# Splitting all seven output products of five head groups on two levels, with five running sums that share two places and wait in DRAM

## The chip, the cores and the metric

The kernel runs on one core of a Trainium2 chip. The metric is the device time of one execution in microseconds (us), lower is better. Before the change the median of three runs was 1238.21 us (1238.15 to 1238.35). The core has five engines, each with a queue of its own that is worked through in order: TensorE (PE in the profile, with its weight loads as PEld), VectorE (DVE), ScalarE (ACT), GpSimd (POOL) and SyncE (SP, which here issues nearly all DMAs). They wait for each other by semaphores only.

## The reference

A layernorm of `x` (2048 rows of 512) goes into an attention with 32 heads of 128 over 2048 cached keys and values, and into a gated MLP; the attention's output projection is multiplied with the SiLU of the MLP and added to `x`.

```python
def _A_ref(x, k_cache, v_cache, wq, wo):
    q = (x @ wq).reshape(B, Sq, H, Dh).transpose(0, 2, 1, 3)
    scores = jnp.einsum("bhqd,bhkd->bhqk", q, k_cache) * (Dh ** -0.5)
    p = _softmax(scores, axis=-1)
    o = jnp.einsum("bhqk,bhkd->bhqd", p, v_cache)
    return o.transpose(0, 2, 1, 3).reshape(B, Sq, H * Dh) @ wo
...
xn = _layernorm(x, axis=-1)
s = _A_ref(xn, A_k_cache, A_v_cache, A_wq, A_wo)
g = _silu(_B_ref(xn, B_W_gate, B_W_up, B_W_down))
return x + s * g
```

The change is in the last product of `_A_ref`, with `wo`.

## The kernel before

**Blocks.** The attention is cut into 128 blocks: block `b` is head `b // 4` and one quarter of the 2048 queries. In a block, 8 pairs of key tiles (steps `p` = 0 to 7) run one after the other: two score matmuls of 512 columns (`emit_S_tile`, L1575), one exponential on ScalarE (L1587), and eight value matmuls (`emit_PV_tile`, L1684). Scores run three pairs ahead of the values. At a block's end VectorE normalizes it (`emit_norm_block`) and SP transposes it into `OT_store` (L1612).

**The ring.** Scores and all other products share a ring of three places in PSUM, two banks each. TensorE takes the next place in turn (`ring_acquire`) and waits until what was in it has been read. `emit_x` and `emit_unit` hold a place over several steps, so that two are left for the scores.

**Head groups.** Four heads (16 blocks) make a group, 8 groups in all. The output product of group `g` runs in the blocks of the next one, which begin at `b0 = 16 * (g + 1)`. In the last group's blocks (112 to 127) the product of group 6 runs. Beside it run the query products of the group to come, in seven "units" of two levels (`emit_unit`), which GpSimd prepares (`prep_unit`) and in two cases adds up (`add_unit`, L1124); the last of these is in block 112.

**The output product.** It is a 2 x 2 product after Strassen and Winograd: seven products 1 to 7 instead of eight. Products 2, 6, 5 and 3 are split once more into seven (`emit_x` with 5 matmuls in steps 0, 2 and 3 of a block, `emit_xd` with 2 in the next block); GpSimd prepares their operands (`prep_x`, L1442). Products 1, 7 and 4 are on one level (`emit_one`): four quarters of two matmuls each. VectorE adds each result to running sums in SBUF, `s_acc`, which has 4 places of 4 x 512 values per partition (1 MB each): place 0 is product 2, place 1 product 6, place 2 product 3, place 3 product 5, and the products on one level go to two places each (`one_to`). `os_tok` holds, for each place and piece, the semaphore value that its next user waits for. A helper `acc` writes the sums (L1377 for 1024 elements, L1389 for 512).

**The order.** Nothing is scheduled while the kernel runs: `plan` and `side` are tables from (block, step) to work, written out by hand at the end of the kernel. At each (block, step) the loop issues the scores three pairs ahead, the items of `plan`, the items of `side`, and the values. `side` items that only SP or GpSimd executes have no time of their own: they stand in that engine's queue behind what was issued before, and start when their semaphores allow it.

**The end.** From block 115, step 5, `reload_g` lets SP load the MLP's result and `x` transposed (`gT`, `xT`: eight transposes) and a part of it plain (`gN`). `emit_finish` and `emit_base` then join the running sums; the last group's own product is done directly.

Of the kernel before, what the change touches and what calls it, by code (L numbers as in the profile page):

```python
# [30 lines left out]
def _wait(eng, tok):  # L31
    if tok is None:
        return
    sem, val = tok
    if val <= 0:
        return
    eng.wait_ge(sem.h, val)


def _wait_all(eng, toks):  # L40
    best = {}
    for t in toks:
        if t is None:
            continue
        sem, val = t
        k = id(sem)
        if k not in best or best[k][1] < val:
            best[k] = (sem, val)
    for sem, val in best.values():
        _wait(eng, (sem, val))  # L50


def bass_recurrent_scan__mha_block_cached__glu_gated_reglu__prompt_kernel(
# [63 lines left out]
    with ExitStack() as es:  # L117
# [35 lines left out]
        def at_(off, shape, dt, name):  # L153
            _cnt[0] += 1
            return nc.alloc_sbuf_tensor_at(f"{name}_{_cnt[0]}", shape, dt, offset=base[0] + off)
# [59 lines left out]
            (104448, 105472, 106496, 107520), (65536, 66560, 100352, 101376)))  # L215
        SI, SJ = (at_(o, [128, 4, Dh], F16, "SI") for o in (102400, 108544))
        SO = at_(88064, [128, 4, DC // 2, 2, Dh], F16, "SO")
        fin_tmp = [WX[1][:, k].rearrange("p h d -> p (h d)").bitcast(BF16) for k in range(4)]
        gT = at_(g_at - base[0], [128, DC, S], BF16, "gT")
        gN = at_(104448, [128, 4, D], BF16, "gN")  # L220
# [35 lines left out]
        sem_uw = newsem()  # L256
        sem_oi = newsem()
        sem_oa = newsem()
        sem_ft = [[newsem(16) for _ in range(2)] for _ in range(QB - 1)]
        sem_hl = newsem(16)  # L260
        sem_wx = newsem()
# [134 lines left out]
        def t_toks(g, c):  # L396
            return [(sem_ob[i], 16 * TPB * (g + 1)) for i in range(NON) if i % 2 == c]
# [932 lines left out]
        def emit_ox(g, c, i):  # L1330
            O, O16 = OT_store[g % 2], OT16[g % 2]
            lo = slice(c * NQ, (c + 1) * NQ)
            hi = slice(HS + c * NQ, HS + (c + 1) * NQ)
            a11, a12 = O[:, 0:GH, lo], O[:, GH:G, lo]
            a21, a22 = O[:, 0:GH, hi], O[:, GH:G, hi]
            s1, s2, s3 = O16[:, 0:GH, hi], OX[1][:, :, lo], OX[0][:, :, lo]
            if i == 0:
                _wait_all(dve, t_toks(g, c) + [os_tok.get("x0")])
                ox_tok["k"] = sem_ox.sig(dve.tensor_tensor(s3, a11, a21, ALU.subtract))
            elif i == 1:  # L1340
                _wait(dve, ox_tok["k"])
# [23 lines left out]
        def acc(J, i, src, op=ALU.add, spread=None):  # L1365
            keys = [(x, y) for x in (J if isinstance(J, tuple) else (J,)) for y in (i if isinstance(i, tuple) else (i,))]
            pair = len(src.shape) == 3
            t = None
            if len(keys) == 2 and all(k in os_tok for k in keys):
                _wait_all(dve, [os_tok[k] for k in keys])  # L1370
                (J0, i0), (J1, i1) = keys
                if J0 != J1:
                    dst = s_acc[:, J0:J1 + 1:J1 - J0, i0, :]
                else:
                    dst = s_acc[:, J0, i0:i1 + 1:i1 - i0, :]
                sb = src if pair else src.unsqueeze(1).to_broadcast([128, 2, NQ])
                t = sem_opa.sig(dve.tensor_tensor(dst, dst, sb, op))  # L1377
                for k in keys:
                    os_tok[k] = t
                return t  # L1380
            for n, k in enumerate(keys):
                dst, sb = s_acc[:, k[0], k[1], :], src[:, n, :] if pair else src
                if spread is not None:
                    _wait_all(act, [spread, d_done[3]])
                    t = os_tok[k] = sem_oa.sig(act.copy(dst, sb))
                    continue
                if k in os_tok:
                    _wait(dve, os_tok[k])
                    t = dve.tensor_tensor(dst, dst, sb, op)  # L1389
                else:  # L1390
                    t = dve.tensor_copy(dst, sb)
                t = os_tok[k] = sem_opa.sig(t)
            return t

        one_to = {1: (0, 1), 7: (1, 2), 4: (1, 3)}
        two_to = {2: 0, 6: 1, 3: 2, 5: 3}

        def emit_one(g, j, r, e0, *banks):
            if j == 1 and r == 0 and e0 == 0:
# [36 lines left out]
        def prep_x(g, j, part):  # L1436
            a11, a12, a21, a22 = (o_a(g, j, i, r) for r in range(2) for i in range(2))
            b11, b12, b21, b22 = (o_b(g, j, i, e) for i in range(2) for e in range(2))
            Z, Y = TO, SJ

            def op(dst, x, y, o=ALU.subtract):
                return sem_oi.sig(pool.tensor_tensor(dst, x, y, o))  # L1442

            if part == 0:
                _wait_all(pool, {2: lambda: [(sem_ob[i], 16 * TPB * (g + 1)) for i in (0, 1)], 6: lambda: [ox_tok[(g, 0)], ox_tok[(g, 1)]],
                                 5: lambda: [ox_tok[(g, 0)], ox_tok[(g, 1)]], 3: lambda: [ox_tok[(g, "4")]]}[j]()
                          + [os_tok.get("c"), sem_dg.cur()])
                k1 = op(Z[0][:], a21, a22, ALU.add)
                op(Z[2][:], a11, a21)
                _wait(pool, k1)  # L1450
                k1 = op(Z[1][:], Z[0][:], a11)
                _wait(pool, k1)
                op(Z[3][:], a12, Z[1][:])
            else:
                _wait_all(pool, [os_tok.get("d"), wx_tok[(g, 0 if j < 4 else 1)]])
                k2 = op(Y[:, 0], b12, b11)
                op(Y[:, 2], b22, b12)
                _wait(pool, k2)
                k2 = op(Y[:, 1], b22, Y[:, 0])
                _wait(pool, k2)  # L1460
                x_prep[(g, j)] = op(Y[:, 3], b21, Y[:, 1])
# [40 lines left out]
        def emit_xd(g, j, *banks):  # L1502
            J = two_to[j]
            sub = ALU.subtract if g == NG - 2 and j == 3 else ALU.add
            pe.matmul(ps_r[:, banks[0], :], o_b(g, j, 1, 0), o_a(g, j, 1, 0), start=True, stop=True)  # L1505
            p = sem_op.sig(pe.matmul(ps_r[:, banks[1], :], SJ[:, 3, :], o_a(g, j, 1, 1), start=True, stop=True))  # L1506
            os_tok["d"] = p
            if j == 6:
                os_tok["6d"] = p
            if j == 3:  # L1510
                os_tok["x1"] = p
            _wait(dve, p)
# [309 lines left out]
        def put_p0(b, it):  # L1822
            assert b not in osteps
            osteps[b] = it
            if it[0] is emit_x or it[0] is emit_xd or it[1] == 1:
                early.add(b)

        xsteps = (0, 2, 3)
        for g in range(NG - 1):
            b0 = (g + 1) * GB  # L1830
            half = g < NG - 2
            split = {} if g == 0 else {3: 6} if half else {3: 5, 8: 4}
            if g == 0:
                full, part, xs = {0: (1, 0), 12: (1, 1), 2: (7, 0), 6: (7, 1)}, (1, 3, 7, 13), {2: 4, 6: 8, 5: 10, 3: 14}
# [80 lines left out]
            elif o:  # L1915
                at(b, 0, o)
        for n, (g, j, b) in enumerate(unit_at):
            first = (1, 3, 5, 6) if osteps[b][0] is emit_xd else (1, 3, 5, 6)
            second = (5, 7) if b + 1 in x_at else (3, 6) if b + 1 in early else (3, 6)
            for step, (r, p) in enumerate([(0, p) for p in first] + [(1, p) for p in second]):  # L1920
                at(b + r, p, (emit_unit, 0, n, step))
            side.setdefault((b - 2, 6), []).append((prep_unit, n, 0))
            side.setdefault((b - 1, 7), []).append((prep_unit, n, 1))
            if j in (5, 7):
                side.setdefault((b + 1, 6), []).append((add_unit, g, j))
        side.setdefault((GB + 1, 0), []).append((spill_g,))
        side.setdefault((LB - 9, 5), []).append((reload_g,))
        for g in range(2, NG):
# [159 lines left out]
```

## Time and profile before

| What | us |
|---|---|
| median of three runs | 1238.21 |
| the profiled execution's own time | 1237.93 |
| its span, first to last instruction | 1236.6 |
| blocks 0 to 15, with the MLP's products, and what precedes them | up to 274.6 |
| blocks 16 to 31 (product of group 0) | 141.4 |
| blocks 32 to 111 (groups 1 to 5), each 16 blocks | 135.4 |
| blocks 112 to 127 (group 6) and the end | from 1093.0 |

Times in the views are microseconds from the span's start. The table by windows gives, for each stretch, the busy time of every engine with its count of instructions, the granted TensorE clock (PEclk), the share of time that the DMA engines were busy, and GB/s. In the timeline a row is: start, duration, engine, line, operation, output and inputs, count, and in brackets the idle time before it with what ended it. A row with a count of more than one runs from the start of the first to the end of the last. In the groups of the page a row has count, total busy time, mean duration in ns, and the engine's idle time before these instructions. Matmuls are pipelined: one of 512 columns shows 379 ns, though the next starts earlier. A block begins, here, with its first value matmul: block 112 at 1093.0, 113 at 1101.4, 114 at 1110.0, 115 at 1118.4, 118 at 1142.1.

### The profile page before, as it was taken

How to read it: one execution, taken by the hardware profiler on the slowest of the kernel's cores; microseconds unless marked ns; L12 is line 12 of the kernel's file. 1: busy time of each engine (PE TensorE's matmuls, PEld its weight loads, DVE VectorE, ACT ScalarE, POOL GpSimd, SP SyncE). 2: the span in 40 equal slices, each digit the busy share in tenths (PEclk: the TensorE clock that was granted, in tenths of full speed). 3: DMA queues.
4: the chain of work that ended last, by engine and by line, in shares of the span. 5: the costliest groups of instructions: out<-in, count | busy, mean ns of one | idle time of the engine just before them, and what ended most of it. 6: DMA issues, size and time to landing. Idle time of an engine off the chain costs nothing.

```text
span 1236.6 us, 28887 instructions
## 1 busy us (share of the span) xinstructions
PE 1219.1 (99%) x11723; PEld 818.7 (66%) x11937; DVE 874.0 (71%) x1311; ACT 1040.8 (84%) x1111; POOL 730.4 (59%) x840
## 2 busy tenths in 40 slices
PE   9999999999999999999999999999999999999998
PEld 5466666776666666666666666666666666666665
DVE  7668787666676767676776777676776677675587
ACT  4457877668899998989999999999999999989994
POOL 3355876313757557755866565846775576662368
PEclk9999999999999999999999999999999999999999
DMA  9712331223223332233122322234222323237526
GB/s 277 157 31 37 80 78 23 52 48 97 52 50 52 65 70 52 49 69 61 40 36 52 74 61 52 48 70 70 48 53 52 52 49 48 52 69 143 110 35 142
DMA packets 279012, 85.25 MB, mean 69 GB/s; under 512 B 253024, under 2 KB 278880, under 8 KB 278880
## 3 DMA queue, kind: packets, MB, share of 16 engines
q1 hardware_dynamic: 277536, 82.61, 34.1%
q8 instruction: 95, 1.56, 0.6%
q10 hardware_dynamic: 1344, 0.79, 0.2%
q14 instruction: 37, 0.30, 0.1%
HBM read 36.96 MB, written 4.19 MB: 33 GB/s over the span
## 4 chain that ended last, share of the span: by engine, by line
PE 97%; issue 1%; ACT 1%; DVE 0%; DMA 0%; SPq 0%; DVEq 0%
PE ps_acc L1684 37%; PE ps_r L1575 34%; PE ps_r L1051 5%; PE ps_r L1168 3%; PE ps_r L1411 3%; PE ps_r L1229 3%; PE ps_r L1474 2%; PE ps_r L915 2%; PE ps_r L734 2%; PE ps_r L730 2%; PE ps_acc L833 1%; PE ps_r L1716 1%; ACT PT L1587 1%; PE ps_r L1505 1%; PE ps_r L1506 1%
## 5 line engine op out<-in xcount | busy, mean ns | idle before, releaser
L1587 ACT ACTIVATE PT<-ps_r 128x1024 bf16<-128x1024 f32 x1024 | 988.6, 1026 | 129.8 <-PE ps_r L1575 116.7
L1684 PEld LDWEIGHTS ps_acc<-V_sb,PT 128*128 128x128 bf16 x8192 | 546.1, 98 | 229.6 <-issue 27.9
L1684 PE MATMUL ps_acc<-V_sb,PT 128*128 128x129 bf16 x8192 | 632.4, 220 | 1.0
L1575 PE MATMUL ps_r<-QT_sb,KT_sb 128*128 128x512 bf16 x1849 | 557.5, 379 | 9.5
L1056 DVE TENSOR_TENSOR UVR<-UVR,ps_r 128x512 f32<-128x512 f32 (+1 forms) x228 | 168.5, 755 | 80.6 <-PE ps_r L1051 78.4
L1377 DVE TENSOR_TENSOR s_acc<-s_acc,ps_r 128x1024 f32<-128x1024 f32 x130 | 156.7, 1218 | 34.0 <-PE ps_r L1411 22.6
L1575 PEld LDWEIGHTS ps_r<-QT_sb,KT_sb 128*128 128x128 bf16 x2048 | 162.7, 98 | 25.5 <-ACT PT L1587 0.3
L1016 POOL TENSOR_TENSOR TI<-xn_sb 128x512 f16<-128x512 f16 x48 | 55.8, 1163 | 95.3 <-PE ps_r L1051 95.3
L1389 DVE TENSOR_TENSOR s_acc<-s_acc,ps_r 128x512 f32<-128x512 f32 x116 | 77.4, 685 | 22.4 <-PE ps_r L1474 17.9
L1607 DVE TENSOR_TENSOR Onorm<-ps_acc,rz_sb 128x512 bf16<-128x512 f32 x127 | 87.8, 691 | 4.4
L1604 DVE RECIPROCAL rz_sb<-ps_acc 128x4 f32<-128x4 f32 x127 | 23.1, 182 | 88.3 <-PE ps_acc L1684 86.8
L1056 DVE TENSOR_TENSOR QT_sb<-UVR,ps_r 128x512 bf16<-128x512 f32 x72 | 49.5, 687 | 50.3 <-PE ps_r L1051 47.9
L1442 POOL TENSOR_TENSOR TI<-OX 128x512 f16<-128x512 f16 x28 | 31.8, 1156 | 65.1 <-issue 65.1
L1016 POOL TENSOR_TENSOR TI<-xnT 128x512 f16<-128x512 bf16 x36 | 41.6, 1156 | 37.5 <-PE ps_r L1051 19.2
L1323 POOL TENSOR_TENSOR WX<-Wo_sb 128x512 f16<-128x512 bf16 x7 | 8.1, 1155 | 90.2 <-DVE Wo_sb L1313 51.2
L1016 POOL TENSOR_TENSOR TI<-xn_sb,TI 128x512 f16<-128x512 f16 x48 | 55.9, 1165 | 0.0
L1124 POOL TENSOR_TENSOR QT_sb<-UVR,UVR 128x512 bf16<-128x512 f32 x24 | 29.8, 1274 | 39.9 <-DVE UVR L1056 39.9
L1051 PE MATMUL ps_r<-TI,SI 128*128 128x512 f16 x126 | 47.8, 379 | 0.4
L1124 POOL TENSOR_TENSOR UVR<-UVR,UVR 128x512 f32<-128x512 f32 x24 | 29.8, 1271 | 27.1 <-DVE UVR L1056 27.1
L1016 POOL TENSOR_TENSOR TI<-xnT,TI 128x512 f16<-128x512 bf16 x36 | 41.6, 1156 | 0.0
L1144 POOL TENSOR_SCALAR gB<-gB 128x512 bf16<-128x512 bf16 x14 | 20.8, 1484 | 30.4 <-DVE gB L1174 30.4
L1442 POOL TENSOR_TENSOR TI<-OT_store 128x512 f16<-128x512 bf16 (+1 forms) x28 | 32.1, 1168 | 9.9 <-issue 9.2
(233 smaller groups left out, 1352.7 us busy)
## 6 DMA issues: line engine op xcount, KB each, us to landing
V_sb<-in_A_v_cache_dram SPq DMA_DIRECT2D x32, 512.0 KB, 4.2
Wq_sb<-in_A_wq_dram SPq DMA_DIRECT2D x16, 256.0 KB, 3.1
Wo_sb<-in_A_wo_dram SPq DMA_DIRECT2D x8, 512.0 KB, 4.6
out_dram<-g_sb SPq DMA_DIRECT2D x4, 512.0 KB, 4.7
OT_store<-Onorm SPq DMA_TRANSPOSE x127, 2.5
Wd_sb<-in_B_W_down_dram SPq DMA_DIRECT2D x1, 1792.0 KB, 14.0
W<-in_B_W_gate_dram SPq DMA_DIRECT2D x14, 128.0 KB, 2.4
W<-in_B_W_up_dram SPq DMA_DIRECT2D x14, 128.0 KB, 2.7
```

The costliest lines, as they stand in the source:

```text
L1016: return sem_ui.sig(pool.tensor_tensor(dst, x, y, o))
L1051: return sem_up.sig(pe.matmul(dst, lhs, rhs, start=start, stop=stop, skip_group_check=True))
L1056: dve.tensor_tensor(dst, x, ps, ALU.add))
L1124: u_tok["add"] = u_tok[("add", i)] = sem_uv.sig(pool.tensor_tensor(dst, UU[:, i, :], RR[:, i, :], ALU.add))
L1168: ins = pe.matmul(ps_r[:, bank, :], L(i), R(i), start=(i == 0), stop=(i == HC - 1))
L1377: t = sem_opa.sig(dve.tensor_tensor(dst, dst, sb, op))
L1389: t = dve.tensor_tensor(dst, dst, sb, op)
L1442: return sem_oi.sig(pool.tensor_tensor(dst, x, y, o))
L1575: ins = pe.matmul(ps_r[:, 2 * s + tt, :], KT_sb[h % 2][:, t * 128:(t + 1) * 128], QT_sb[qt_slot[(h, Q)]][:], start=True, stop=True)
L1587: act.activation(PT[pb][:], ps_r[:, 2 * s:2 * s + 2, :], ACTF.Exp, scale=scale / WSC)
L1607: dve.tensor_tensor(Onorm[ob][:], o_ap, rz_sb[:].to_broadcast([128, 4, Dh]), ALU.mult))
L1684: ins = pe.matmul(o_ap, PT[pb][:, tt, j * 128:(j + 1) * 128], V_sb[vb][:, t, 0:VW], start=(t == 0 and j % 2 == 0), stop=(t == KT - 1 and j ...
```

## The change

In groups 1 to 5 (`half and g` in the plan) products 1, 7 and 4 are split on two levels as well. Each then has a running sum of its own, so there are seven sums `a` = 0 to 6 (4, 5 and 6 are products 1, 7 and 4), of which 0 and 1 keep a place, and five share places 2 and 3 (`SLOT`). What is not in its place lies in DRAM (`swap`): `store_sum` and `load_sum` move one sum of 1 MB on SP's queue, at hand-written places. The order in a group is 2, 1, 7, 6, 4, 5, 3, in blocks 0, 2, 4, 6, 8, 10 and 14.

In the last group's blocks the three sums 4, 5 and 6 come back into `RR` (`load_kept`), which the last `add_unit` has just read, and GpSimd adds each to the two running sums that the product on one level goes to (`add_kept`, 8 additions of 512 elements).

Beside this, part 1 of `prep_unit` moves from (b - 1, 7) to (b, 3), `add_unit` moves to (b + 2, 0) where the next block has an `emit_x`, and the first of the four `emit_ox` pieces waits for the first two heads only.

```diff
+        SLOT = (0, 1, 2, 3, 2, 3, 2)
+        swap = {a: nc.dram_tensor(f"sums{a}", [128, 4 * NQ], F32).ap() for a in (2, 3, 4, 5, 6)}
...
-        two_to = {2: 0, 6: 1, 3: 2, 5: 3}
+        two_to = {2: 0, 6: 1, 3: 2, 5: 3, 1: 4, 7: 5, 4: 6}
+        slot_free = {}
+        kept = {}
+
+        def store_sum(a):
+            k = SLOT[a]
+            _wait_all(sp, [os_tok[(a, i)] for i in range(4)])
+            slot_free[k] = kept[a] = sem_as[k].sig(
+                sp.dma_start(swap[a], s_acc[:, k].rearrange("p i q -> p (i q)")))
+
+        def load_sum(a):
+            k = SLOT[a]
+            _wait_all(sp, [slot_free[k], kept[a]])
+            t = sem_al[k].sig(sp.dma_start(s_acc[:, k].rearrange("p i q -> p (i q)"), swap[a]))
+            for i in range(4):
+                os_tok[(a, i)] = t
+
+        def load_kept(a):
+            _wait_all(sp, [kept[a], u_tok["add"], os_tok.get("rr")])
+            os_tok["rl"] = sem_rr.sig(sp.dma_start(RR[:].rearrange("p i q -> p (i q)"), swap[a]))
+
+        def add_kept(a):
+            _wait(pool, os_tok["rl"])
+            for J in one_to[{4: 1, 5: 7, 6: 4}[a]]:
+                for i in range(4):
+                    _wait(pool, os_tok[(J, i)])
+                    d = s_acc[:, J, i, :]
+                    os_tok[(J, i)] = os_tok["rr"] = sem_fo.sig(pool.tensor_tensor(d, d, RR[:, i, :], ALU.add))
...
+            if half and g:
+                order = ((2, 0), (1, 2), (7, 4), (6, 6), (4, 8), (5, 10), (3, 14))
+                left[g] = len(order)
+                for j, r in order:
+                    x_at.add(b0 + r)
+                    put_p0(b0 + r, (emit_x, 0, g, j, 0))
+                    for k in (1, 2):
+                        at(b0 + r, xsteps[k], (emit_x, 0, g, j, k))
+                    put_p0(b0 + r + 1, (emit_xd, 2, g, j))
+                    side.setdefault((b0 + r - 2, 4), []).append((prep_x, g, j, 0))
+                    side.setdefault((b0 + r - 1, 1), []).append((prep_x, g, j, 1))
...
+                moves = [((4, 1), store_sum, 4), ((6, 1), store_sum, 5), ((7, 2), load_sum, 3), ((10, 1), store_sum, 6),
+                         ((11, 2), load_sum, 2)]
+                if g == 1:
+                    moves += [((-2, 1), store_sum, 3), ((0, 1), store_sum, 2)]
+                else:
+                    moves += [((1, 2), load_sum, 4), ((-3, 2), load_sum, 5), ((5, 2), load_sum, 6)]
+                if g < NG - 3:
+                    moves += [((12, 1), store_sum, 3), ((16, 1), store_sum, 2)]
...
-            side.setdefault((b - 1, 7), []).append((prep_unit, n, 1))
+            side.setdefault((b, 3), []).append((prep_unit, n, 1))
             if j in (5, 7):
-                side.setdefault((b + 1, 6), []).append((add_unit, g, j))
+                side.setdefault((b + 2, 0) if b + 1 in x_at else (b + 1, 6), []).append((add_unit, g, j))
...
         fb = GB * (NG - 1)
+        for r, a in ((1, 4), (3, 5), (5, 6)):
+            side.setdefault((fb + r, 0), []).append((load_kept, a))
+            side.setdefault((fb + r, 6), []).append((add_kept, a))
```

More of the change, by code (lines that the diff above doesn't have):

```diff
@@ L258, in bass_recurrent_scan__mha_block_cached__glu_gated_reglu__prompt_kernel @@
         sem_oa = newsem()
+        sem_as = {k: newsem(16) for k in (2, 3)}
+        sem_al = {k: newsem(16) for k in (2, 3)}
+        sem_rr = newsem(16)
+        sem_fo = newsem()
         sem_ft = [[newsem(16) for _ in range(2)] for _ in range(QB - 1)]
@@ L1337, in emit_ox @@
             if i == 0:
-                _wait_all(dve, t_toks(g, c) + [os_tok.get("x0")])
-                ox_tok["k"] = sem_ox.sig(dve.tensor_tensor(s3, a11, a21, ALU.subtract))
+                early_toks = [(sem_ob[q], 16 * (TPB * g + GH)) for q in range(NON) if q % 2 == c]
+                _wait_all(dve, early_toks + [os_tok.get("x0")])
+                ox_tok[(g, c, 0)] = ox_tok["k"] = sem_ox.sig(dve.tensor_tensor(s3, a11, a21, ALU.subtract))
             elif i == 1:
-                _wait(dve, ox_tok["k"])
+                _wait_all(dve, t_toks(g, c) + [ox_tok["k"]])
                 ox_tok["k"] = sem_ox.sig(dve.tensor_tensor(s1, a21, a22, ALU.add))
@@ L1374, in acc @@
                 else:
-                    dst = s_acc[:, J0, i0:i1 + 1:i1 - i0, :]
+                    dst = s_acc[:, SLOT[J0], i0:i1 + 1:i1 - i0, :]
                 sb = src if pair else src.unsqueeze(1).to_broadcast([128, 2, NQ])
@@ L1381, in acc @@
             for n, k in enumerate(keys):
-                dst, sb = s_acc[:, k[0], k[1], :], src[:, n, :] if pair else src
+                dst, sb = s_acc[:, SLOT[k[0]], k[1], :], src[:, n, :] if pair else src
                 if spread is not None:
@@ L1390, in acc @@
                 else:
+                    _wait(dve, slot_free.get(SLOT[k[0]]))
                     t = dve.tensor_copy(dst, sb)
@@ L1445, in prep_x @@
                 _wait_all(pool, {2: lambda: [(sem_ob[i], 16 * TPB * (g + 1)) for i in (0, 1)], 6: lambda: [ox_tok[(g, 0)], ox_tok[(g, 1)]],
-                                 5: lambda: [ox_tok[(g, 0)], ox_tok[(g, 1)]], 3: lambda: [ox_tok[(g, "4")]]}[j]()
+                                 5: lambda: [ox_tok[(g, 0)], ox_tok[(g, 1)]], 3: lambda: [ox_tok[(g, "4")]],
+                                 1: lambda: [(sem_ob[i], 16 * (TPB * g + GH)) for i in (0, 1)],
+                                 7: lambda: [ox_tok[(g, 0, 0)], ox_tok[(g, 1, 0)]],
+                                 4: lambda: [(sem_ob[i], 16 * TPB * (g + 1)) for i in (2, 3)]}[j]()
                           + [os_tok.get("c"), sem_dg.cur()])
@@ L1511, in emit_xd @@
                 os_tok["x1"] = p
+            if j == 7:
+                os_tok["x0"] = p
             _wait(dve, p)
@@ L1831, in bass_recurrent_scan__mha_block_cached__glu_gated_reglu__prompt_kernel @@
             half = g < NG - 2
+            if half and g:
[9 more added lines that the diff above has]
+                    side.setdefault((b0 + r - 1, 1), []).append((prep_x, g, j, 1))
+                for (r, p), c, i in (((-2, 2), 0, 0), ((-2, 6), 1, 0), ((3, 2), 0, 1), ((3, 3), 0, 2), ((3, 4), 1, 1),
+                                     ((3, 6), 1, 2), ((8, 1), 0, 3), ((8, 5), 1, 3)):
+                    side.setdefault((b0 + r, p), []).append((emit_ox, g, c, i))
+                moves = [((4, 1), store_sum, 4), ((6, 1), store_sum, 5), ((7, 2), load_sum, 3), ((10, 1), store_sum, 6),
[6 more added lines that the diff above has]
+                    moves += [((12, 1), store_sum, 3), ((16, 1), store_sum, 2)]
+                for (r, p), fn, a in moves:
+                    side.setdefault((b0 + r, p), []).append((fn, a))
+                continue
             split = {} if g == 0 else {3: 6} if half else {3: 5, 8: 4}
@@ L1917, in bass_recurrent_scan__mha_block_cached__glu_gated_reglu__prompt_kernel @@
         for n, (g, j, b) in enumerate(unit_at):
-            first = (1, 3, 5, 6) if osteps[b][0] is emit_xd else (1, 3, 5, 6)
+            first = (1, 3, 5, 6)
             second = (5, 7) if b + 1 in x_at else (3, 6) if b + 1 in early else (3, 6)
```

## The prediction

> **What bounds the kernel now.** I read the page's span, busy shares and chain first, then the table by windows, one window for each head group, and then the timeline of the last group.
>
> ```profile
> span 1236.6 us, 28887 instructions
> PE 1219.1 (99%) x11723; PEld 818.7 (66%) x11937; DVE 874.0 (71%) x1311; ACT 1040.8 (84%) x1111; POOL 730.4 (59%) x840
> PE 97%; issue 1%; ACT 1%; DVE 0%; DMA 0%; SPq 0%; DVEq 0%
> ```
>
> ```profile
> core 0: us, PE busy (x) PEld busy (x) DVE busy (x) ACT busy (x) POOL busy (x), PEclk, DMA share, GB/s
> 551.34:686.75 135.41, 134.07 (x1358) 91.83 (x1381) 95.30 (x136) 123.65 (x129) 86.82 (x105) 1.00 0.28 56
> 686.75:822.17 135.42, 134.07 (x1358) 91.80 (x1381) 95.49 (x136) 123.67 (x129) 86.81 (x105) 1.00 0.29 56
> ```
>
> The chain is TensorE for 97%, and two successive groups take 135.41 and 135.42 us. TensorE issues without a gap, so a matmul taken out of a group should shorten it by its price. The price of one is the distance between two starts, not its duration:
>
> ```profile
> 1141.28 1.03 PE L1411 MATMUL ps_r<-OX,WX 128*128 128x512 f16 x4
> ```
>
> ```profile
> L1051 PE MATMUL ps_r<-TI,SI 128*128 128x512 f16 x126 | 47.8, 379 | 0.4
> ```
>
> Four product matmuls together take 1.03 us (timeline), one alone 0.38 (page), so (1.03 - 0.38) / 3 = 0.217 us.
>
> The other side of this tightness: any wait of TensorE is added to the time in full.
>
> **What the change takes away.** A product on one level is 2 x 2 quarters of 2 matmuls, 8 in all; on two levels it is 5 in `emit_x` and 2 in `emit_xd`, 7. Products 1, 7 and 4 of five groups change: 15 matmuls, 15 x 0.217 = 3.3 us. That is the whole gain.
>
> **What it adds beside TensorE.** VectorE (the sums in groups 1 to 5): a product on one level is four sums of 1024 elements, on two levels two of 1024 and four of 512.
>
> ```profile
> L1377 DVE TENSOR_TENSOR s_acc<-s_acc,ps_r 128x1024 f32<-128x1024 f32 x130 | 156.7, 1218 | 34.0 <-PE ps_r L1411 22.6
> L1389 DVE TENSOR_TENSOR s_acc<-s_acc,ps_r 128x512 f32<-128x512 f32 x116 | 77.4, 685 | 22.4 <-PE ps_r L1474 17.9
> L1442 POOL TENSOR_TENSOR TI<-OX 128x512 f16<-128x512 f16 x28 | 31.8, 1156 | 65.1 <-issue 65.1
> ...
> L1442 POOL TENSOR_TENSOR SI<-WX,SI 128x128 f16<-128x128 f16 x4 | 1.7, 430 | 0.2
> ```
>
> 4 x 1.218 = 4.9 becomes 2 x 1.218 + 4 x 0.685 = 5.2 us, three times a group: 0.9 us on 95 of 135. GpSimd prepares three more products, each four pieces of 1.156 us and four small ones of 0.43 us (the last row is of one group's view by lines), 6.3 us: 87 becomes 106 of 135. Both stay under TensorE, in blocks already as dense in the old schedule (4 to 7, 10, 11, 14, 15), so I cost them at nothing. Without that cover the worst place is block 12, where the preparation of product 3 now stands ahead of `add_unit`: about 0.2 us a group.
>
> DMA: 25 stores and 25 loads of 1 MB, up to 10 MB in a group that moves 135 us x 56 GB/s = 7.6 MB now. The engines have moved 330 GB/s in this trace, so volume is not the limit:
>
> ```profile
> 3.40:7.00 3.60, 2.93 (x34) 2.00 (x32) 3.33 (x10) 1.23 (x3) 0.00 (x0) 1.00 1.06 330
> ```
>
> **A load's duration.** No 1 MB load is in the trace. Nearest rows:
>
> ```profile
> V_sb<-in_A_v_cache_dram SPq DMA_DIRECT2D x32, 512.0 KB, 4.2
> Wo_sb<-in_A_wo_dram SPq DMA_DIRECT2D x8, 512.0 KB, 4.6
> Wd_sb<-in_B_W_down_dram SPq DMA_DIRECT2D x1, 1792.0 KB, 14.0
> W<-in_B_W_gate_dram SPq DMA_DIRECT2D x14, 128.0 KB, 2.4
> ```
>
> It is not under 4.2 (half the bytes) and not over 14.0 (1.75 times the bytes, while the input loads crowd the queues). From 2.4 at 128 KB to 4.2 at 512 KB is 1.8 us for 384 KB; another 512 KB is 2.4 more: 6.6, I take 6.5. The Trainium skill (SBUF — State Buffer, "The DMA setup-cost knee") puts a transfer at 2 us and its bytes at 436 GB/s, so an estimate of 4.4 us here; by that rule the total below would be about 4 us less. The trace does not agree with it for 512 KB: 4.2 to 4.6 against its 3.2.
>
> In groups 2 to 5 the sum of product 1 is loaded behind the transpose of block 0 of the group and needed by the first sum of block 2. In the group that begins at 686.75:
>
> ```profile
> 1118.30 1.19 SPq L1612 DMA_TRANSPOSE OT_store<-Onorm  x1
> ...
> 695.04 9.82 SPq L1612 DMA_TRANSPOSE OT_store<-Onorm  x2
> ...
> 703.60 2.35 DVE L1377 TENSOR_TENSOR s_acc<-s_acc,ps_r 128x1024 f32<-128x1024 f32 x2
> ```
>
> Issue at 695.0 + 1.2 = 696.3 (one such transpose occupies SP's queue for 1.19 us, first row), landing at 702.8, needed at 703.6; TensorE asks for the sum some 2 us later still. I cost it at nothing; above a load of 9 us it costs a microsecond for each microsecond, four times.
>
> **What it adds on the path: two waits in the last group.** Three kept sums (4, 5, 6) are loaded into `RR` and added by GpSimd to two running sums each, 8 additions. VectorE's next sum of the same places must wait for GpSimd; behind it in VectorE's queue stand all others, and `emit_one`'s place in the ring of three is given back only when they are done.
>
> First wait, block 114. `RR` is free when `add_unit` of the last unit ends.
>
> ```profile
> 1099.79 4.97 POOL L1124 TENSOR_TENSOR QT_sb<-UVR,UVR 128x512 bf16<-128x512 f32 x4 [6.66 <-DVE UVR L1056]
> ```
>
> ```profile
> L1124 POOL TENSOR_TENSOR UVR<-UVR,UVR 128x512 f32<-128x512 f32 x24 | 29.8, 1271 | 27.1 <-DVE UVR L1056 27.1
> ```
>
> ```profile
> 1109.85 2.35 DVE L1377 TENSOR_TENSOR s_acc<-s_acc,ps_r 128x1024 f32<-128x1024 f32 x2
> ...
> 1109.22 1.03 PE L1411 MATMUL ps_r<-OT_store,Wo_sb 128*128 128x512 bf16 x4
> ...
> 1110.54 0.59 PE L1575 MATMUL ps_r<-QT_sb,KT_sb 128*128 128x512 bf16 x2
> ...
> 1112.31 0.59 PE L1575 MATMUL ps_r<-QT_sb,KT_sb 128*128 128x512 bf16 x2
> ```
>
> SP can issue load 4 at 1099.79 + 4.97 = 1104.8; it lands at 1111.3. GpSimd's additions follow each other every (4.97 - 1.27) / 3 = 1.23 us: the sixth, which VectorE's first sum needs, ends at 1118.7, the eighth, for the second sum, at 1121.2. VectorE, which did both from 1109.85, ends the second at 1122.4. TensorE has two pairs of scores left in the other two places (1110.54 and the next); the third, at 1112.31, needs the place of `emit_one`. It waits from 1112.3 to 1122.4: **10.1 us**. Nothing hides it, since ScalarE is fed by these scores alone.
>
> Second wait, block 118. Product 7's second half adds to sums 1 and 2, and `add_kept(6)`, written one step ahead of it, owns sum 1. Load 6 stands in SP's queue behind `reload_g`, and behind the transposes of blocks 115 and 116.
>
> ```profile
> 1121.76 1.99 SPq L357 DMA_TRANSPOSE KT_sb<-in_A_k_cache_dram  x1
> 1123.86 1.59 SPq L1137 DMA_TRANSPOSE gT<-out_dram  x1
> 1125.49 3.50 SPq L1138 DMA_TRANSPOSE xT<-in_A_x_dram  x1
> ...
> 1145.54 4.66 SPq L1612 DMA_TRANSPOSE OT_store<-Onorm  x1
> ...
> 1150.24 2.57 SPq L1612 DMA_TRANSPOSE OT_store<-Onorm  x2
> ...
> 1141.91 2.35 DVE L1377 TENSOR_TENSOR s_acc<-s_acc,ps_r 128x1024 f32<-128x1024 f32 x2
> ...
> 1144.36 0.59 PE L1575 MATMUL ps_r<-QT_sb,KT_sb 128*128 128x512 bf16 x2
> ```
>
> The list from KT (which waits for scores of block 115, so it moves with the first wait) to the end of the second transpose lasts 1150.24 + 1.3 - 1121.76 = 29.8 us. On the old clock load 6 is issued at 1151.5 and lands at 1158.0; sum 1 comes first: its second addition ends at 1160.5, its fourth at 1162.9, VectorE's second sum 1.2 later at 1164.1. TensorE wants the place at 1144.36: **19.7 us**. Load 5 with its additions is done some 15 us earlier and decides nothing.
>
> Restart. After standing still TensorE begins at half pace in this trace:
>
> ```profile
> 0.76 3.40 PE L476 MATMUL ps_r<-const-bfloat16-1.0 128*128 128x256 bf16 x18 [0.76 <-PEq L2073]
> L476 PE MATMUL ps_r<-const-bfloat16-1.0 x21: 273/418/418, 0.8 to 5.0; 128*128 128x256 bf16 x21
> ```
>
> At full pace 256 columns are half of 0.217 us apart, so 18 would take 17 x 0.108 + 0.27 = 2.1 us; they take 3.4: 1.3 us lost, and the durations (418 against 273 ns) show it though the granted clock reads 1.00. Ends: 0 and 2.5. I take 1.3 for each wait, 2.6. The Trainium skill (TensorE: Matmul & The Clock Gate, "What's actually happening") says that the array falls to half clock after an idle window of 3.4 us and stays there for one busy window; by that each restart costs 1.7, and the total is 0.8 higher. No run here shows a stop in mid-kernel.
>
> **Sum.** On the profiled execution: 1237.93 (span 1236.6 and 1.3 around it) - 3.3 + 10.1 + 19.7 + 2.6 = 1267.0. The median shown is 0.3 above that execution: 1267.3; I say 1267 us.
>
> **Rivals.**
> A shorter list in SP's queue (chance 0.11). While TensorE stands, no head is loaded; if the transposes of `reload_g` were then issued at 1.2 us each, like the small ones, ten entries would take 15 us less, the second wait 5: 1252. For it: their queue times differ (1.59 for one, 3.50 for the next). Against: they carry the same bytes, and the queue is full of themselves.
>
> The sums come in time (0.06), the faster side. One mechanism: kept sums are added before VectorE asks. It decides if load 4 and six additions are through by 1112.3 - 2.4 = 1109.9, 5.1 us after `RR` is free. Six additions alone are 7.4 us by the rows, so only additions at half that price, or an earlier end of the last unit, would do it; likewise for load 6. Price: both waits and restarts gone, 1238.2 - 3.3 = 1235 us.
>
> Loads are late in the groups too (0.09). At 14.0 us, the row under load, block 2 of four groups waits 14.0 - 9 = 5 us, and each tail wait grows by 7.5: 1267 + 20 + 15 = 1302. Against: 56 GB/s in these windows.
>
> The change does not do what it says (0.04): TensorE keeps its 135.4 us a group, with the additions hidden: 1238. For it: ScalarE is busy for 124 of 135 us. Against: it idles 12.
>
> **Chances and range.** Forecast with both waits 0.70. Its own ends: loads of 4.2 (-4.6), no queueing in front of load 6 beyond 1.2 us (-3.4) and no slow restart (-2.6) give 1256; loads of 9.2, twice the Wo row, give +5.4 and restarts of 2.5 another 2.4: 1275. With the short list below, 1250 to 1276. 0.2% (2.5 us) is about what a measurement can tell from no change: faster 0.06, same 0.04, slower 0.90.
>
> **What would show it.** Right: groups of 134.8 us (135.42 - 0.65); in block 114 a gap of about 10 us on TensorE ended by VectorE's sum, which is ended by GpSimd; a second, longer one in block 118, with load 6 issued after the last transpose of `reload_g`. Wrong: loads under 4 or over 9 us, TensorE running on past three pairs of scores, or groups still at 135.4.

## The result, and the profile after

The changed kernel takes 1281.53 us (median of 5 runs, 1280.43 to 1282.35) against 1238.21 for the kernel before (5 runs, 1238.13 to 1239.41): a ratio of 1.0348, 95% interval 1.0333 to 1.0363. It is 43.3 us slower. The prediction said slower, at 1267 us and not beyond 1276; it is 14.5 us too low.

The page of the changed kernel: its span, the busy shares, the granted clock in 40 slices of 32 us, and the chain.

```profile
span 1280.2 us, 29335 instructions
PE 1237.6 (97%) x11922; PEld 818.9 (64%) x11922; DVE 892.7 (70%) x1344; ACT 1044.6 (82%) x1111; POOL 860.4 (67%) x984
...
PEclk9999999999999999999999999999999999987999
...
PE 90%; DVE 2%; SPq 2%; POOL 2%; issue 1%; DMA 1%; ACT 1%; DVEq 0%; POOLq 0%
```

TensorE is still the chain, but for 90% and no longer 97%: VectorE, SP's queue and GpSimd have come into it, and in slices 36 and 37, the last group, the granted clock falls. The groups of the page say what TensorE now waits for.

```profile
L1724 PE MATMUL ps_acc<-V_sb,PT 128*128 128x129 bf16 x8192 | 633.5, 221 | 6.6 <-DVE Onorm L1647 6.6
L1615 PE MATMUL ps_r<-QT_sb,KT_sb 128*128 128x512 bf16 x2048 | 606.3, 381 | 28.1 <-DVE s_acc L1384 27.9
```

28 us stand in front of the scores, for VectorE's sums. They are the two waits in the last group that the prediction described. The 6.6 us in front of the values, for the normalization (`Onorm`), it had not foreseen. The table by windows for two of the changed head groups, cut at the weight loads of their first value matmuls:

```profile
core 0: us, PE busy (x) PEld busy (x) DVE busy (x) ACT busy (x) POOL busy (x), PEclk, DMA share, GB/s
553.59:690.52 136.93, 135.38 (x1380) 91.18 (x1378) 97.64 (x141) 124.30 (x129) 106.97 (x129) 1.00 0.49 132
690.52:827.46 136.94, 135.39 (x1380) 91.20 (x1379) 98.16 (x141) 124.31 (x129) 106.82 (x129) 1.00 0.53 132
```

136.93 instead of 135.42. A group has not become 0.65 us shorter but 1.51 longer. Where the 43.6 us between the two profiled executions (1281.53 and 1237.93) lie is told by the next table. Its cuts are the weight loads of the blocks' first value matmuls, as in all times of blocks here and ahead; the matmul itself mostly starts some 0.1 us later.

| Stretch | before | after | difference | forecast |
|---|---|---|---|---|
| blocks 16 to 31 | 141.35 | 141.94 | +0.6 | 0 |
| groups 1 to 5 | 677.1 | 684.7 | +7.6 | -3.3 |
| block 114 | 8.38 | 19.80 | +11.4 | +11.4 |
| block 118 | 7.96 | 30.43 | +22.5 | +21.0 |
| after the last value matmul | 8.5 | 9.9 | +1.4 | 0 |

The forecast column has 1.3 us of restart in each of the two blocks. The last row is SP's: its last three transposes of the output take 4.53 us in this execution and 3.85 in the old one, and the last store follows later. No run was made on that, and the cause stays open. It is hardly chance: in the profiles of the eight experiments below that contain the change this stretch takes 9.2 to 10.3 us, and in experiment 7, which does not contain it, 8.4.

**The waits in the last group.** The timeline of the changed kernel, first for block 114 (1118.4 to 1138.2), then for block 118 (1161.9 to 1192.3):

```profile
1113.20 0.34 SPq L1423 DMA_DIRECT2D UVR<-sums  x1
...
1118.12 9.82 POOL L1431 TENSOR_TENSOR s_acc<-s_acc,UVR 128x512 f32<-128x512 f32 x8 [2.38 <-DMA UVR<-sums]
...
1125.60 1.22 DVE L1384 TENSOR_TENSOR s_acc<-s_acc,ps_r 128x1024 f32<-128x1024 f32 x1 [7.31 <-POOL s_acc L1431]
1128.04 1.22 DVE L1384 TENSOR_TENSOR s_acc<-s_acc,ps_r 128x1024 f32<-128x1024 f32 x1 [1.22 <-POOL s_acc L1431]
...
1129.32 1.03 PE L1615 MATMUL ps_r<-QT_sb,KT_sb 128*128 128x512 bf16 x2 [8.46 <-DVE s_acc L1384]
...
1144.51 2.29 SPq L1143 DMA_TRANSPOSE gT<-out_dram  x1
...
1166.68 5.31 SPq L1652 DMA_TRANSPOSE OT_store<-Onorm  x2
1172.11 0.50 SPq L1423 DMA_DIRECT2D UVR<-sums  x1
...
1177.50 10.71 POOL L1431 TENSOR_TENSOR s_acc<-s_acc,UVR 128x512 f32<-128x512 f32 x8 [16.69 <-DMA UVR<-sums]
...
1180.08 1.22 DVE L1384 TENSOR_TENSOR s_acc<-s_acc,ps_r 128x1024 f32<-128x1024 f32 x1 [18.31 <-POOL s_acc L1431]
...
1183.80 1.03 PE L1615 MATMUL ps_r<-QT_sb,KT_sb 128*128 128x512 bf16 x2 [19.46 <-DVE s_acc L1384]
```

Read it backwards: the score matmul waits for VectorE, VectorE for GpSimd, GpSimd for a load, and the second load was issued behind `reload_g` and two more transposes. (`RR` appears as `UVR`, whose memory it shares.)

**The waits in the groups.** The timeline of TensorE at the start of block 12 of a changed group, with VectorE's normalization of block 11:

```profile
790.85 0.62 PE L1724 MATMUL ps_acc<-V_sb,PT 128*128 128x129 bf16 x8
791.30 0.59 PE L1615 MATMUL ps_r<-QT_sb,KT_sb 128*128 128x512 bf16 x2
...
791.51 0.18 DVE L1644 RECIPROCAL rz_sb<-ps_acc 128x4 f32<-128x4 f32 x1 [0.65 <-PE ps_acc L1724]
791.72 0.69 DVE L1647 TENSOR_TENSOR Onorm<-ps_acc,rz_sb 128x512 bf16<-128x512 f32 x1
...
792.56 0.61 PE L1724 MATMUL ps_acc<-V_sb,PT 128*128 128x129 bf16 x8 [0.66 <-DVE Onorm L1647]
793.01 0.59 PE L1615 MATMUL ps_r<-QT_sb,KT_sb 128*128 128x512 bf16 x2
793.44 0.62 PE L1724 MATMUL ps_acc<-V_sb,PT 128*128 128x129 bf16 x8
```

The same place in the kernel before:

```profile
786.71 0.62 PE L1684 MATMUL ps_acc<-V_sb,PT 128*128 128x129 bf16 x8
787.16 1.03 PE L1575 MATMUL ps_r<-QT_sb,KT_sb 128*128 128x512 bf16 x4
788.02 0.59 PE L1411 MATMUL ps_r<-OT_store,WX 128*128 128x512 bf16 x2
788.46 1.07 PE L1684 MATMUL ps_acc<-V_sb,PT 128*128 128x129 bf16 x16
```

The values of a new block overwrite the accumulator that the normalization reads, so between the last values of a block and the first of the next TensorE needs other work. From the rows of after, it needs 792.56 - 791.30 = 1.26 us. Before, two pairs of scores and two product matmuls stand there: 788.46 - 787.16 = 1.30 us, just enough. After, one pair: the next instruction could start 0.43 us after it (as from 793.01 to 793.44), so some 0.82 us are lost, of which the row shows 0.66, because matmul ends are modelled. Seven split products take 14 of the 16 blocks of a group, and blocks 12 and 13 have none. Both the product's matmuls and the second pair of scores go with it, since the loop issues that pair ahead only at a step 0 that has an item from `put_p0`. The list of waits gives this wait ten times in all, two for each of five groups.

A third, smaller one is in block 14, where the first `emit_ox` pieces now stand between VectorE's sums:

```profile
813.07 0.69 DVE L1346 TENSOR_TENSOR OX<-OT_store 128x1024 f16<-128x1024 bf16 x1
813.67 1.21 DVE L1384 TENSOR_TENSOR s_acc<-s_acc,ps_r 128x1024 f32<-128x1024 f32 x1
...
814.94 0.39 PE L1057 MATMUL ps_r<-TI,SI 128*128 128x512 f16 x1 [0.22 <-DVE s_acc L1384]
```

VectorE's sum of product 3 begins 0.6 us later, and TensorE waits for its place in `ps_r`: block 14 takes 8.99 us instead of 8.59, 9.42 in one group.

So a group is 2 x 0.82 + 0.40 (block 14) + 0.13 (block 4, not examined) - 0.65 (three matmuls less) = +1.52, as measured.

### The profile page after: what moved, and what is told of

The parts are those of the page before. It is cut to its first block, busy times and chain, and to the rows that moved or that the text cites. A ratio compares the mean times of both kernels' runs of the same rounds, so it can differ in the third digit from the quotient of the medians.

```text
span 1280.2 us, 29335 instructions
## 1 busy us (share of the span) xinstructions
PE 1237.6 (97%) x11922; PEld 818.9 (64%) x11922; DVE 892.7 (70%) x1344; ACT 1044.6 (82%) x1111; POOL 860.4 (67%) x984
## 4 chain that ended last, share of the span: by engine, by line
PE 90%; DVE 2%; SPq 2%; POOL 2%; issue 1%; DMA 1%; ACT 1%; DVEq 0%; POOLq 0%
PE ps_acc L1724 34%; PE ps_r L1615 32%; PE ps_r L1057 5%; PE ps_r L1512 3%; PE ps_r L1174 3%; PE ps_r L1235 3%; PE ps_r L921 2%; PE ps_r L736 2%; PE ps_r L740 2%; POOL s_acc L1431 1%; PE ps_acc L839 1%; SPq L1144 1%; PE ps_r L1756 1%; PE ps_r L1543 1%; SPq L1143 1%
## 5 line engine op out<-in xcount | busy, mean ns | idle before, releaser
L1615 PE MATMUL ps_r<-QT_sb,KT_sb 128*128 128x512 bf16 x2048 | 606.3, 381 | 28.1 <-DVE s_acc L1384 27.9
L1384 DVE TENSOR_TENSOR s_acc<-s_acc,ps_r 128x1024 f32<-128x1024 f32 x97 | 117.9, 1219 | 48.2 <-POOL s_acc L1431 28.1
L1396 DVE TENSOR_TENSOR s_acc<-s_acc,ps_r 128x512 f32<-128x512 f32 x170 | 113.5, 686 | 30.2 <-PE ps_r L1512 23.8
L1477 POOL TENSOR_TENSOR TI<-OT_store 128x512 f16<-128x512 bf16 (+1 forms) x48 | 54.8, 1162 | 52.9 <-issue 24.8
L1477 POOL TENSOR_TENSOR TI<-OX 128x512 f16<-128x512 f16 x38 | 43.1, 1155 | 48.5 <-issue 48.5
L1431 POOL TENSOR_TENSOR s_acc<-s_acc,UVR 128x512 f32<-128x512 f32 x24 | 30.4, 1308 | 29.6 <-DMA UVR<-sums 29.6
L1057 PE MATMUL ps_r<-TI,SI 128*128 128x512 f16 x126 | 48.1, 381 | 1.1 <-DVE s_acc L1384 1.1
L1512 PE MATMUL ps_r<-TI,SI 128*128 128x512 f16 x129 | 48.9, 379 | 0.0
L1150 POOL TENSOR_SCALAR gB<-gB 128x512 bf16<-128x512 bf16 x14 | 20.8, 1484 | 30.4 <-DVE gB L1180 30.4
```

The source lines that it names most:

```text
L1057: return sem_up.sig(pe.matmul(dst, lhs, rhs, start=start, stop=stop, skip_group_check=True))
L1431: os_tok[(J, i)] = os_tok["rr"] = sem_fo.sig(pool.tensor_tensor(d, d, RR[:, i, :], ALU.add))
L1512: return sem_op.sig(pe.matmul(dst, lhs, rhs, start=start, stop=stop, skip_group_check=True))
L1615: ins = pe.matmul(ps_r[:, 2 * s + tt, :], KT_sb[h % 2][:, t * 128:(t + 1) * 128], QT_sb[qt_slot[(h, Q)]][:], start=True, stop=True)
```

## The experiments

**1. Both tail waits undone.** GpSimd adds sum 4 later and in the order that VectorE leaves the places, and sum 6 only behind product 7:

```diff
         for r, a in ((1, 4), (3, 5), (5, 6)):
             side.setdefault((fb + r, 0), []).append((load_kept, a))
-            side.setdefault((fb + r, 6), []).append((add_kept, a))
+        for r, p, a, *Js in ((2, 2, 4, 1, 0), (3, 6, 5), (7, 1, 6, 3), (9, 5, 6, 1)):
+            side.setdefault((fb + r, p), []).append((add_kept, a, *Js))
```

`add_kept` takes the places `Js` as arguments, and the four `emit_base(0, i)` move two blocks later, to blocks 120 and 121. The `diff` shown here, and in the experiments below, is the main part of the edit.

> Only the last group's order differs from the changed kernel: GpSimd adds the kept sums where no sum of VectorE needs the same place soon (sum 4 after product 1's second half, its second place first; sum 6 to place 3 after block 119 step 0 and to place 1 after block 121 step 4), and four emit_base pieces stand two blocks later. Theory (the two waits are the program order of add_kept against VectorE's sums): blocks 114 and 118 go from 19.8 and 30.4 us back to 8.4 and 8.0, the granted clock stays at 1.00 throughout, and the time falls by 11.4 + 22.5 = 33.9 from 1281.5 to 1247.6 us. Rival (the kept loads themselves, 3 MB beside the transposes of reload_g, hold the tail up): blocks 112 to 120 stay over 8.5 us each and the time stays over 1255. The groups stay at 136.9 us by both.

Measured: 1257.18 us (1256.99 to 1257.93), ratio 1.0155 (1.0140 to 1.0170). Blocks 114 and 118 are back at 8.38 and 7.96, and the groups stay at 136.54 to 137.30. But 10 us are lost anew in blocks 115 to 122; the last 16 blocks take 145.2 us against 135.2 in the kernel before. Nor does the granted clock stay at 1.00: a wait of 3.69 us in block 121, for GpSimd, comes with another stretch at half clock (0.51 from 1188.7 to 1195.6). The timeline of this kernel, SP, GpSimd and VectorE:

```profile
1132.95 0.34 SPq L1423 DMA_DIRECT2D UVR<-sums  x1
1133.35 4.58 SPq L363 DMA_TRANSPOSE KT_sb<-in_A_k_cache_dram  x1
1138.04 2.96 SPq L1143 DMA_TRANSPOSE gT<-out_dram  x1
...
1161.34 6.19 SPq L1652 DMA_TRANSPOSE OT_store<-Onorm  x2
1167.65 0.50 SPq L1423 DMA_DIRECT2D UVR<-sums  x1
...
1173.37 5.85 POOL L1431 TENSOR_TENSOR s_acc<-s_acc,UVR 128x512 f32<-128x512 f32 x4 [19.01 <-DMA UVR<-sums]
...
1168.28 0.18 DVE L1644 RECIPROCAL rz_sb<-ps_acc 128x4 f32<-128x4 f32 x1 [7.11 <-DMA OT_store<-Onorm]
```

SP stands still for the load of sum 5 until GpSimd has done with sum 4, and all behind it, `reload_g` and the transposes of `Onorm`, is late: KT is issued 6.4 us behind the start of block 115, instead of 3.4. The theory gave the two waits and the groups right; that the rest of the tail would be undisturbed was wrong, and the rival (the tail held up by its loads) took 10 us of the 34 back. Experiments 3, 8 and 9 tell how much of that is bytes and how much order.

**2. The second wait alone undone.** As experiment 1, but sum 4 is added where the change has it.

```diff
+        for r, p, a, *Js in ((1, 6, 4), (3, 6, 5), (7, 1, 6, 3), (9, 5, 6, 1)):
```

> The changed kernel with the second wait alone undone: sum 6 is added to place 3 after block 119 step 0 and to place 1 after block 121 step 4, four emit_base pieces stand two blocks later; the first wait and SP's order are as in the changed kernel. Theory (the waits are independent, each its idle time and a restart at half clock): block 114 stays at 19.8 us, block 118 falls from 30.4 to 8.0, the time from 1281.5 by 22.5 to 1259. Rival (the kept loads stand on the path whatever the order of the additions): the wait moves to blocks 119 to 122 and the time stays over 1270. In e1_tail the waits of blocks 119 to 122 came to 10 us because SP stood 6 us longer ahead of reload_g for load 5; here SP is not held longer than in the changed kernel.

Measured, in 2 runs: 1262.21 us (1261.78 to 1262.63), ratio 1.0196 (1.0175 to 1.0216). Block 118 is back at 7.96, block 114 has 18.92, and blocks 121 and 123 take 3.7 us longer than before. The two waits are separate: undoing one leaves the other.

**3. The sums moved without their bytes.** As experiment 1, but each store and load moves 16 of 2048 columns, so the parked sums are not restored.

```diff
-                sp.dma_start(swap[a], s_acc[:, k].rearrange("p i q -> p (i q)")))
+                sp.dma_start(swap[a][:, 0:16], s_acc[:, k, 0, 0:16]))
```

> e1_tail with every store and load of a sum, the kept ones too, cut to 16 of 2048 columns: same DMAs in number, order and waits, hardly any bytes; the sums that come out are not those of the reference. Theory (the bytes cost nothing): groups stay at 136.9 us, 1247.6 in all. Rival (50 MB more traffic is what lengthens the groups): groups at 135 us or less, about 1238.

Measured, in one run: 1251.48 us. The groups take the same 136.9 us, at 55 GB/s instead of 132. The 50 MB cost the groups nothing. The last 16 blocks go from 145.2 to 139.1: beside `reload_g`, in this order, the bytes do cost, 6 us.

**4. The cover in blocks 12 and 13.** As experiment 1, and at step 0 of these blocks the next pair of scores is issued ahead, as in the others.

```diff
+            if pq == 0 and bq in bare:
+                s_ahead.add(gp + 1)
+                emit_S_pair(gp + 1)
             if items:
```

`bare` holds blocks 12 and 13 of the five groups.

> e1_tail, and at the start of blocks 12 and 13 of groups 1 to 5, which have no product at step 0 any more, the next pair of scores is issued ahead, as the other blocks do it. Theory (the groups grew because in these two blocks TensorE has one pair of scores, 0.43 us, to do while VectorE normalizes the block before, and waits 0.8 us): the wait falls by a pair, 0.43 us, in each of the ten blocks: groups 136.9 to 136.1 us, 4.3 us less than e1_tail, 1243.3. Rivals (stores and loads of sums in the way of other traffic; GpSimd's additions behind the preparation of product 3): nothing changes, 1247.6.

Measured: 1252.54 us (1251.79 to 1253.02), ratio 1.0116 (1.0101 to 1.0131): 4.6 us less than experiment 1. A group loses 0.43 us for each of the two blocks, which is a pair of scores, and two pairs (0.87) still leave 1.26 - 0.87 = 0.39 us of wait.

**5. The first `emit_ox` pieces two blocks earlier.** As experiment 1 otherwise.

```diff
-                for (r, p), c, i in (((-2, 2), 0, 0), ((-2, 6), 1, 0), ((3, 2), 0, 1), ((3, 3), 0, 2), ((3, 4), 1, 1),
+                for (r, p), c, i in (((-4, 2), 0, 0), ((-4, 5), 1, 0), ((3, 2), 0, 1), ((3, 3), 0, 2), ((3, 4), 1, 1),
```

> e1_tail, and the first piece of emit_ox for the next group moves from block 14 (steps 2 and 6) to block 12 (steps 2 and 5), where VectorE is idle. Theory (in block 14 it stands between product 3's sums in VectorE's queue and holds the ring): block 14 falls from 9.0 (9.4 in the last such group, 9.25 in group 0's) to 8.6, together about 2.5 us less than e1_tail, 1245. Rival (block 14 is long for another reason, such as GpSimd's late preparation): no change, 1247.6.

Measured: 1254.09 us (1254.00 to 1255.42), ratio 1.0133 (1.0116 to 1.0150): 3.1 us less. Block 14 takes 8.59 us in every group, blocks 16 to 31 are back at 141.35, and groups take 136.54.

**6. Blocks 12 and 13 filled.** Experiments 1, 4 and 5 together, and one unit matmul is moved to step 0 of block 12, two to that of block 13.

```diff
-            first = (1, 3, 5, 6)
+            first = (0, 3, 5, 6) if b in bare else (1, 3, 5, 6)
```

`second` has (0, 6) where block b + 1 is in `bare`.

> e1_tail with e3_cover and e4_ox together, and the query units of blocks 11 and 13 moved so that one matmul of theirs stands at step 0 of block 12 and two at step 0 of block 13. Theory: TensorE then has 0.65 and 0.86 us beside the normalization and the rest of the 0.82 us waits goes: groups from 136.54 (e4_ox) to about 134.9 us, under the 135.42 of before, so the 15 matmuls show at last; the tail stays at 144 us; 1254.1 - 8.2 = 1246. Rival (the groups are long for another reason as well): groups stay over 135.4, time over 1248.

Measured: 1246.66 us (1246.18 to 1247.74), ratio 1.0071 (1.0056 to 1.0086). The table by windows of this kernel:

```profile
551.20:686.32 135.12, 135.11 (x1380) 91.27 (x1378) 99.79 (x141) 124.12 (x129) 107.43 (x129) 1.00 0.49 134
```

135.12 us, under the old 135.42, with the same split products and the same traffic, and the list of waits names none of TensorE in the groups. So covers and `emit_ox` explain the growth of the groups. Of the 0.65 us that three matmuls are worth, though, only 0.30 show. At the start of block 12 TensorE still has 1.25 us between the same two points (787.11 to 788.36 in this kernel's timeline) and only five matmuls, 1.08 us, to fill them: 0.17 us. The 0.13 in block 4 stays as well. What remains above the old time is the tail, 144.1 us.

**7. The same wait put into the kernel before.** In block 13 of groups 1 to 5 the next pair is not issued ahead; nothing else differs from the old kernel.

```diff
-            if it[0] is emit_x or it[0] is emit_xd or it[1] == 1:
+            if (it[0] is emit_x or it[0] is emit_xd or it[1] == 1) and b not in (45, 61, 77, 93, 109):
                 early.add(b)
```

> The kernel before, and nothing of the change: in block 13 of groups 1 to 5 alone (five blocks of 128) the next pair of scores is no longer issued ahead at step 0; the two product matmuls there stay. Theory (a block's start needs some 1.3 us of work of TensorE beside the normalization of the block before: two pairs of scores and two matmuls, 0.43 us each, and what is missing is waited for): each of the five blocks grows from 8.62 to about 9.0 us, 2.1 us in all, 1240.2. Rival (the blocks of the changed kernel waited for something that the change brought, its sums, its GpSimd work or its DMAs): no change, 1238.1.

Measured: 1239.89 us (10 runs, 1239.72 to 1241.03) against 1238.26, ratio 1.0012 (1.0003 to 1.0021). The timeline of this kernel at the start of block 13:

```profile
796.98 0.59 PE L1575 MATMUL ps_r<-QT_sb,KT_sb 128*128 128x512 bf16 x2
797.41 0.59 PE L1411 MATMUL ps_r<-OT_store,WX 128*128 128x512 bf16 x2
798.23 0.61 PE L1684 MATMUL ps_acc<-V_sb,PT 128*128 128x129 bf16 x8 [0.23 <-DVE Onorm L1607]
```

798.23 - 796.98 = 1.25 us again, now with one pair and two product matmuls (0.87) inside. The rest is a wait, and a group takes 135.77, 0.35 more. The cover is a property of the loop, not of the split products.

**8. and 9. The tail.** Experiment 8 is experiment 6, with the loads of the kept sums issued from GpSimd's queue, each behind the additions that free `RR`, so SP waits for none of them. In experiment 9, moreover, sum 5 is added odd pieces first, and `reload_g` is cut in halves, in blocks 115 and 116.

```diff
-            _wait_all(sp, [kept[a], u_tok["add"], os_tok.get("rr")])
-            os_tok["rl"] = sem_rr.sig(sp.dma_start(RR[:].rearrange("p i q -> p (i q)"), swap[a]))
+            _wait_all(pool, [kept[a], u_tok["add"], os_tok.get("rr")])
+            os_tok["rl"] = sem_rr.sig(pool.dma_start(RR[:].rearrange("p i q -> p (i q)"), swap[a]))
```

> e6_filled, and the three kept loads are issued from GpSimd's queue, each right behind the additions that free the buffer, so that SP never stands for them and reload_g starts as early as before the change. Theory (what is left in the tail is SP's queue held by a load's wait: reload_g, the transposes and load 6 come late): blocks 112 to 127 fall from 144 to 136 to 138 us, 1238 to 1240 in all. Rival (3 MB beside reload_g's transposes, bytes and not order): the tail stays over 141, time over 1243.

> e7_pool with two orders changed in the last group: sum 5 is added to the pieces first that product 7's second half needs in block 118, and reload_g is split in two, so that the transpose of block 115 goes between its halves and the normalization of block 119 finds it done. Theory (what is left of the tail's excess is these two waits, 12.2 and 9.9 us in blocks 118 and 121 against 8.0 and 8.4): blocks 112 to 127 fall from 141.3 to about 136 us, the time from 1244.9 to about 1239.5: the groups' gain, 5 x 0.3 us, is then as good as all that is left of the 15 matmuls, and lies within what can be measured. Rival (the 3 MB of kept loads slow reload_g's transposes, so the wait only moves on): the tail stays over 139, time over 1242.

Measured: 1244.88 us (1242.89 to 1246.40), ratio 1.0056 (1.0039 to 1.0072), and 1239.63 us (11 runs, 1238.93 to 1240.05) against 1238.26 (21 runs), ratio 1.0008 (0.9999 to 1.0017). The first came out where its rival had it (the tail over 141 us, the time over 1243), but experiment 9, which loads the same bytes, shows that most of it is order. In experiment 8 VectorE met GpSimd's additions of sum 5 in block 118 (12.16 us instead of 7.96), and at the end of block 119 (8.25 instead of 7.65) it stood for a transpose that waited in SP's queue:

```profile
1160.36 0.18 DVE L1644 RECIPROCAL rz_sb<-ps_acc 128x4 f32<-128x4 f32 x1 [5.73 <-DMA OT_store<-Onorm]
```

In the second both are gone, and only block 121 (9.87 in both kernels, 8.44 before) is left. There no transpose is waited for. VectorE is busy without a pause, and two of the `emit_base` sums that experiment 1 moved (L1578) now stand ahead of the normalization:

```profile
1168.52 2.35 DVE L1385 TENSOR_TENSOR s_acc<-s_acc,ps_r 128x1024 f32<-128x1024 f32 x2
1170.79 2.79 DVE L1578 SCALAR_TENSOR_TENSOR s_acc<-s_acc,gT 128x512 f32<-128x512 f32 x2
1173.50 0.17 DVE L1646 RECIPROCAL rz_sb<-ps_acc 128x4 f32<-128x4 f32 x1
```

That this is the whole of block 121's excess was not tested. The groups gain 5 x 0.30 = 1.5 us, the last 16 blocks lose 1.5 (136.7), and from the last value matmul to the end it is 10.2 us (9.9 in the change, 8.5 before). So nearly all of the loss can be taken back by order alone, and what is then left is within what this measurement can tell from no change. No version was faster than the kernel before.

## Why the prediction was wrong, point by point

- **The two waits in the tail: right**, in place and order of events, and near in size. TensorE stood for 8.46 us in block 114 (10.1 forecast) and 19.46 in block 118 (19.7). A kept sum took 5.2 us to load, between the 6.5 taken and the Trainium skill's 4.4 (SBUF — State Buffer, "The DMA setup-cost knee"), which does not hold here:

```profile
sums<-s_acc SPq DMA_DIRECT2D x25, 1024.0 KB, 4.6
s_acc<-sums SPq DMA_DIRECT2D x22, 1024.0 KB, 5.2
...
UVR<-sums SPq DMA_DIRECT2D x3, 1024.0 KB, 5.2
```

- **Two more pairs of scores, then a stop: right.** The last two start at 1118.92 and 1119.81.
- **The restart: mechanism right, term too small.** 1.3 us each was taken, with 2.5 as the upper end; blocks 114 and 118 are longer than their waits by 11.42 - 8.46 = 2.96 and 22.47 - 19.46 = 3.01 us. That is 3.4 us of the error, and the start of the kernel was a poor row for it. It is luck that the tail as a whole is within 1.5 us of the forecast: the waits came out 1.9 us shorter and the restarts 3.4 longer.
- **No load late in the groups, volume free: right**, by experiment 3.
- **"That is the whole gain" and "Both stay under TensorE, in blocks already as dense in the old schedule": the step that failed.** The matmuls are gone, and VectorE and GpSimd do stay below their limits (98 and 107 us of 137). But the forecast priced the blocks that got more work, and not the two that lost it. Blocks 12 and 13 lost their product, with it the pair issued ahead, and so the cover of the normalization: 2 x 0.82 x 5 = 8.2 us. Shown by experiments 4 and 6, which give cover back, and by 7, which takes it away from the old kernel. Even with it back, 1.5 of the 3.3 us of gain show. Block 12 was named as the worst place, but for GpSimd's order and 0.2 us, which the runs don't show. The old trace had the needed row: 1.30 us of TensorE's work where the normalization takes 1.26.
- **The moved `emit_ox` pieces, costed at nothing: wrong by some 2.6 us**, 2.0 in the groups and 0.6 in block 30. Experiment 5 takes 3.1 back. The prediction has no term for them. As load of VectorE there is room for them; what counts is the delay of the sum behind them in its queue.
- The rivals: a shorter list on SP's queue did not come (from KT at 1141.57 to the end of the transposes at 1172.0 it lasted 30.4 us, 29.8 forecast), nor the sums in time, nor late loads; nor did the groups keep their 135.4 us.

The sum of the misses: groups and block 30 +11.5, tail waits and restarts +1.5, the end of the span +1.4, whose cause is open; 14.4 of 14.5.

## What to carry to other kernels

When an edit gathers work into some slots of a dense schedule, price the slots that become empty first: list what ran there, what was issued only because it ran there, and what both covered. An engine with 30% to spare still delays the bound engine when a moved instruction stands ahead of the one that frees a buffer. A transfer that frees and fills a buffer by hand should not wait in a queue on which others depend: here its place in SP's order cost more than its bytes.

## What the runs showed of the hardware

TensorE comes back from a stop of 8 or 19 us at half its clock and stays there for several us. The table by windows of the changed kernel, from the two restarts on:

```profile
1129.30:1131.50 2.20, 2.18 (x12) 1.36 (x13) 0.61 (x1) 1.02 (x1) 2.12 (x3) 0.50 0.00 0
1131.50:1135.00 3.50, 3.50 (x23) 2.40 (x21) 0.08 (x1) 1.76 (x2) 2.57 (x5) 0.50 0.02 5
1135.00:1138.00 3.00, 3.00 (x27) 1.76 (x26) 1.48 (x3) 2.58 (x4) 0.00 (x0) 0.98 0.00 0
1183.80:1186.00 2.20, 2.20 (x12) 1.37 (x13) 2.20 (x2) 1.02 (x1) 2.20 (x2) 0.50 0.00 0
1186.00:1189.00 3.00, 3.00 (x21) 2.16 (x20) 1.09 (x1) 1.71 (x2) 3.00 (x3) 0.50 0.00 0
1189.00:1192.30 3.30, 3.30 (x28) 1.74 (x25) 0.87 (x2) 2.68 (x4) 1.43 (x2) 0.89 0.00 0
```

The granted clock is 0.50 from 1129.3 to about 1135.1 and from 1183.8 to about 1189.7, 5.8 and 5.9 us, and half of that is lost. In experiment 2 the first stop is of the same length (8.55 us), but the clock is back 3.8 us after it and block 114 is 0.9 us shorter, so the length varies. The Trainium skill (TensorE: Matmul & The Clock Gate, "What's actually happening") asks for one busy window of 3.4 us before the full clock returns, and says that the windows run freely and do not begin with the work; the rest of a running window and a whole one behind it are 3.4 to 6.8 us, an estimate from the Trainium skill, and all three restarts lie in it. The 1.7 us that the prediction took from the Trainium skill counted one window alone.
